# Issuing w2 and w1 ahead of wq at the head of a decode kernel's transfer queue

## The chip, the cores and the metric

The kernel runs on one core of a Trainium2 chip. The metric is device time in microseconds (us) of one execution, the median of several runs. The core has a matrix engine (TensorE, PE in the profile; PEld is its weight load), VectorE (DVE), ScalarE (ACT), GpSimd (POOL) and SyncE (SP), each with its own instruction stream, and 16 DMA engines that move data between device memory (HBM) and the on-chip buffer. Engines wait for one another, and for transfers, through semaphores.

## What is computed

One decode step with batch 4, one token each and width 576. A layernorm of x feeds two branches that are added to x: attention with 32 query heads over 16 key/value heads of 128, on the last 2048 of 8192 cached positions, and a mixing MLP. Cut to what matters here (all weights and inputs are bf16):

```python
xn = layernorm(x)                                   # (4, 1, 576)
# branch A
q = (xn @ wq).reshape(B, 1, 32, 128)                # wq (576, 4096)
k, v = k_cache[:, :, -2048:, :], v_cache[:, :, -2048:, :]
p = softmax(q k^T * 128**-0.5);  o = p v            # 2 query heads per KV head
a = o @ wo                                          # wo (4096, 576)
# branch B, on xn
h = gelu(layernorm(xn) @ w1)                        # w1 (576, 576)
hs = shift_along_sequence(h) @ w2                   # w2 (576, 576); shifts by 1 and 2, zeros moved in
x1 = xn + hs
b = x1 + gelu(layernorm(x1) @ w3) @ w4              # w3 (576, 4608), w4 (4608, 576)
out = x + a + b
```

With one token in the sequence every shift moves zeros in, so the operand of w2 in the kernel (hs_inT) is the zeroed tile of line 212. The product with w2 and the one with w1 are both executed.

## The kernel before

Everything but x comes in over one queue, SP's, as large transfers of 128 partitions each, in the order of SP's program: wq in three pieces (two of 2048 KB, each two of the four row groups, and a remainder of 512 KB), w2 and w1 (648 KB each), w3 in three pieces (two of 2304 KB and a remainder of 576 KB), then sixteen K tiles of 2048 KB, sixteen V tiles of 2048 KB with wo (4608 KB) among them, and w4 in five pieces. x is loaded by ACT's queue.

The buffers decide what may be issued when. K has four slots, and K tile g (from the fifth on) waits for the last transpose of tile g - 4 (the waits `T...` in line 237). V has four slots too. Before V comes, wq, w1 and w2 lie in V's slots, so the first V tiles wait for the product with w1, named `hT` (line 241). w3 lies in regB, which later holds the transposed K tiles. The first eight transfers and the first four K tiles wait for nothing.

What sets the order: every operation is added to one engine's list with a sort key (`add`, `add_dma`), and at the end each list is sorted by key and then by the order of adding (line 577). An engine runs its list in that order, and an instruction that waits holds all behind it on the same engine. The keys of the first transfers are -20 and -18 for the halves of wq, -15 for its remainder, -14 for w2, -13 for w1, -12 and -10 for the halves of w3, -8 for its remainder, then 0, 1, 2, ... for the K tiles.

PE's list at the head, in order: the transposes of xn (L294, L297) and of the second layernorm's result (L284); the q product with wq, 40 matmuls in five groups, the first two waiting for wq's first half, the next two for its second half, the last for its remainder (L316, `pe_q`); the eight transposes of q (L327); the product of hs_inT with w2 in two halves of 9 matmuls (`pe_hs`, L497), the product of xn2T with w1 (18 matmuls, L497, `hT`); the transposes of x1n (L294, L297); the product with w3, 60 matmuls in five groups, the first two waiting for w3's first half (24 matmuls), the next two for its second half, the last for its remainder (L528, `pe_h2`); four matmuls that zero the score banks (L341, `zeroS`), which wait for the gelu of the w3 product on ACT (L538); and then the loop over the K tiles: eight groups of eight transposes per tile (L352, `T0` to `T127`), copied out by DVE (L360) and ACT (L359), and the score matmuls (L368). After the scores come the softmax, sixteen groups of 64 matmuls with V (L449), the product with wo (L464) and the product with w4 (L464 for its first 14 row groups, L544 behind them), which ends the kernel with two small copies (L571, L572) and two output transfers.

The chain between the w2 product and the w3 product runs over DVE and ACT: x1 = xn + hs (L507), the third layernorm, transposes on PE, and the copy to x1nT (L512).

Of the kernel before, what the change touches and what calls it, by code (L numbers as in the profile page):

```python
# [38 lines left out]
def bass_parallel_sum__sliding_block_cached__mixer_s_mlp__decode_kernel(  # L39
# [22 lines left out]
    with ExitStack() as ctx:  # L62
# [3 lines left out]
        def sem(name):  # L66
            return ctx.enter_context(nc.semaphore(name))
# [15 lines left out]
        w1p = vring_t[:, _o:_o + 9 * HALF]  # L83
        _o += 9 * HALF
        w2p = vring_t[:, _o:_o + 9 * HALF]
# [79 lines left out]
        def add(engine, emit, waits=(), sig=None, key=0.0, loop=None):  # L165
            seqc[0] += 1
            prog[engine].append(Op(emit, waits, sig, key, seqc[0], loop))

        def add_dma(pairs, skey, waits=(), key=0.0, engine="sp"):
            if skey not in S:  # L170
                S[skey] = sem("s_" + "_".join(str(k) for k in (skey if isinstance(skey, tuple) else (skey,))))
            dma_count[skey] = dma_count.get(skey, 0) + 16 * len(pairs)

            def emit(e):
                for o_, i_ in pairs:
                    e.dma_start(o_, i_).then_inc(S[skey], 16)  # L176
            add(engine, emit, waits, None, key)
            return ("dma", skey, dma_count[skey])
# [42 lines left out]
        ev_wq.append(add_dma([(wqrag, rag_src(A_wq))], ("wq", 4), (), -15))  # L221
        def packed(w):
            return w.rearrange("r n -> (r n)").rearrange("(p e) -> p e", p=128)
        ev_w2 = add_dma([(w2p, packed(B_w2))], "w2", (), -14)
        ev_w1 = add_dma([(w1p, packed(B_w1))], "w1", (), -13)
        w3_src = B_w3[0:512, :].rearrange("(p r) n -> p r n", r=4)
        for r in (0, 2):
            ev_w3 += 2 * [add_dma([(w3main[:, r:r + 2, :], w3_src[:, r:r + 2, :])], ("w3", r), (), -12 + r)]
# [430 lines left out]
```

## Time and profile before

| | us |
|---|---|
| median of three runs | 214.77 |
| lowest and highest | 214.73, 214.99 |
| the profiled execution, whole | 214.88 |
| its span in the profile | 213.6 |
| PE busy | 138.9 (65%) |
| DVE busy | 87.3 (41%) |
| ACT busy | 59.3 (28%) |
| POOL busy | 12.0 (6%) |

How to read it. The profile is of one execution; times count from the start of its span. "L352" is line 352 of the kernel. The slices cut the span into 40 equal parts of 5.34 us; a digit is the busy share of a slice in tenths, 9 for 90% or more. A queue's share is the time that its packets took, as a share of 16 engines' span. The chain of waits goes back from the last instruction to what released it; its pieces are shown as start, duration, what. A row of the timeline has start, duration, engine, line, operation, output<-inputs with their shapes, the number of instructions, and in brackets the idle time ahead of it and what ended that. A row of transfers has the number, KB each, and the us from issue to landing. A row of the windows has for each engine its busy time and number of instructions, then the clock granted to PE (1.00 is full), the DMA share and GB/s.

### The profile page before, as it was taken

Reading aid. Unit: us, or ns where it says so; the run is one execution under the profiler, and the core shown is the slowest. Engines: PE = TensorE matmul, PEld = TensorE weight load, DVE = VectorE, ACT = ScalarE, POOL = GpSimd, SP = SyncE. Lnnn points to the kernel's source line nnn. Section 1 sums busy time; section 2 is a strip of 40 time slices with the busy share of each in tenths; the row PEclk is TensorE's granted clock in tenths of the full one; section 3 lists DMA queues with packets and bytes.
Section 4 is the critical chain, followed back from the end, with each engine's and each line's share of the span. In section 5 each row is a group of like instructions: output and inputs, shape, how many; then the busy total and the mean of one; then the engine's idle time right before and its main releaser. Section 6 shows DMA issues by size and latency. Waiting matters only on the chain.

```text
span 213.6 us, 5830 instructions
## 1 busy us (share of the span) xinstructions
PE 138.9 (65%) x2692; PEld 108.9 (51%) x2692; DVE 87.3 (41%) x162; ACT 59.3 (28%) x72; POOL 12.0 (6%) x39
## 2 busy tenths in 40 slices
PE   0089347999999994999999729823343443333585
PEld 0036123777777883788887503823343443333444
DVE  6725202566666664366666569611111112100000
ACT  2000302466665553266566654000000000000000
POOL 8501000000000100000000000000000000000000
PEclk9999855899999999699999995555555555555579
DMA  6999999999999999999999999999999999999993
GB/s 243 426 404 446 438 412 439 423 422 417 436 426 420 426 439 429 417 433 431 429 417 439 429 429 441 427 417 426 420 433 433 426 420 436 433 417 429 432 408 125
DMA packets 6657, 88.63 MB, mean 415 GB/s; under 512 B 748, under 2 KB 888, under 8 KB 1656
## 3 DMA queue, kind: packets, MB, share of 16 engines
q1 hardware_dynamic: 6632, 88.50, 97.8%
q8 instruction: 7, 0.11, 0.2%
q14 instruction: 2, 0.02, 0.0%
q10 hardware_dynamic: 16, 0.01, 0.0%
HBM read 88.49 MB, written 0.00 MB: 414 GB/s over the span
## 4 chain that ended last, share of the span: by engine, by line
DMA 52%; PE 39%; DVE 4%; issue 2%; SPq 1%; ACT 1%
PE ps L352 23%; DMA vring<-in_A_v_cache_dram 23%; DMA regB<-in_B_w_dram 12%; DMA kring<-in_A_k_cache_dram 8%; DMA vring<-in_B_w_dram 8%; PE ps L368 7%; PE ps L449 4%; PE ps L544 1%; PE ps L528 1%; DVE PTb L402 1%; SPq L176 1%; DVE rmax L394 1%; PE ps L341 1%; DVE regB L360 1%; ACT PTb L538 1%
## 5 line engine op out<-in xcount | busy, mean ns | idle before, releaser
L360 DVE COPY regB<-ps 128x1024 bf16<-128x1024 bf16 x80 | 52.4, 687 | 34.1 <-PE ps L352 32.3
L352 PEld LDWEIGHTS ps<-perm_k,kring 128*128 128x128 bf16 x1024 | 59.2, 100 | 11.6 <-issue 8.2
L352 PE MATMUL ps<-perm_k,kring 128*128 128x128 bf16 x1024 | 62.4, 222 | 3.2 <-DMA kring<-in_A_k_cache_dram 3.1
L359 ACT ACTIVATE regB<-ps 128x1024 bf16<-128x1024 bf16 x48 | 47.7, 1023 | 40.9 <-PE ps L352 40.9
L449 PE MATMUL ps<-PTg,vring 128*128 128x8 bf16 x1024 | 29.5, 168 | 39.0 <-DMA vring<-in_A_v_cache_dram 36.4
L449 PEld LDWEIGHTS ps<-PTg,vring 128*128 128x128 bf16 x1024 | 28.4, 104 | 40.1 <-DMA vring<-in_A_v_cache_dram 27.5
L457 DVE TENSOR_TENSOR PTb<-ps,PTb 128x32 bf16<-128x32 f32 x16 | 3.1, 192 | 56.1 <-PE ps L449 56.1
L368 PE MATMUL ps<-regB,Qs 128*32 128x512 bf16 x272 | 18.7, 396 | 4.6 <-issue 3.5
L554 ACT ACTIVATE P_sb<-ps 100x288 f32<-100x288 f32 x1 | 0.4, 411 | 75.8 <-PE ps L464 75.8
L368 PEld LDWEIGHTS ps<-regB,Qs 128*32 128x32 bf16 x272 | 6.6, 97 | 10.8 <-issue 6.4
L413 DVE TENSOR_TENSOR PTg<-PTs,bmask 128x512 bf16<-128x512 bf16 x16 | 10.7, 682 | 0.0
L390 POOL COPY Qs<-Qpad 128x128 bf16<-128x128 bf16 x16 | 4.6, 296 | 91.3 <-PE ps L368 82.0
L528 PE MATMUL ps<-regB,x1nT 128*32 128x432 bf16 (+1 forms) x60 | 4.4, 459 | 6.0 <-DMA regB<-in_B_w_dram 6.0
L541 DVE STREAM_TRANSPOSE h2T_sb<-PTb 128x1152 bf16<-128x1152 bf16 x1 | 1.4, 1379 | 11.4 <-ACT PTb L538 11.4
L528 PEld LDWEIGHTS ps<-regB,x1nT 128*32 128x32 bf16 x60 | 1.8, 122 | 8.0 <-DMA regB<-in_B_w_dram 6.6
L403 PE MATMUL ps<-PTb,perm_p 128*128 128x512 bf16 x4 | 2.4, 607 | 4.3 <-DVE PTb L402 4.1
L294 PE MATMUL ps<-ident_bf,xn_bf 4*128 4x4 bf16 x4 | 0.3, 166 | 7.5 <-DVE ragsrc L278 7.5
L571 DVE CAST out_sb<-ps 36x144 bf16<-36x144 f32 x1 | 0.3, 301 | 9.9 <-PE ps L544 9.9
L464 PE MATMUL ps<-kring,ORT 128*4 128x288 bf16 x64 | 4.0, 441 | 0.4 <-DVE ORT L478 0.4
L294 PEld LDWEIGHTS ps<-ident_bf,xn_bf 4*128 4x128 bf16 x4 | 0.2, 110 | 7.4 <-POOL ones_f L213 7.4
L316 PE MATMUL ps<-vring,xnT 128*32 128x512 bf16 x40 | 3.9, 571 | 0.0
L403 PEld LDWEIGHTS ps<-PTb,perm_p 128*128 128x128 bf16 x4 | 0.4, 104 | 6.3 <-DVE PTb L402 6.3
(99 smaller groups left out, 79.1 us busy)
## 6 DMA issues: line engine op xcount, KB each, us to landing
kring<-in_A_k_cache_dram SPq DMA_DIRECT2D x16, 2048.0 KB, 15.7
vring<-in_A_v_cache_dram SPq DMA_DIRECT2D x16, 2048.0 KB, 17.6
regB<-in_B_w_dram SPq DMA_DIRECT2D x2, 2304.0 KB, 23.5
kring<-in_A_wo_dram SPq DMA_DIRECT2D x1, 4608.0 KB, 23.6
vring<-in_A_wq_dram SPq DMA_DIRECT2D x2, 2048.0 KB, 9.6
vring<-in_B_w_dram SPq DMA_DIRECT2D x2, 2016.0 KB, 17.4
vring<-in_B_w_dram SPq DMA_DIRECT2D x2, 648.0 KB, 14.3
vring<-in_B_w_dram SPq DMA_DIRECT2D x1, 720.0 KB, 14.4
```

The lines of the kernel that those rows point to most:

```text
L316: ins = e.matmul(Qps[32 * j:32 * j + 32, k, :], lhsT=x_, rhs=w, start=(r == 0), stop=(r == 4), tile_position=(0, 32 * j))
L352: ins = e.transpose(tb[n % NTB][:, t, :], kring[:, g % NKS, 8 * k + t, :], perm_k[:])
L359: return "act", lambda e: e.activation(out=ktbuf[:, n % NKT], in_=src, func=ACTF.Copy)
L360: return "dve", lambda e: e.tensor_copy(out=ktbuf[:, n % NKT], in_=src)
L368: ins = e.matmul(Sps[32 * b:32 * b + 32, c4, :].rearrange("p (t i) -> p t i", t=16), lhsT=Qs[:, g % 4, b, :], rhs=kttile[:, t0:t0 + 16, b, :],
L390: P(lambda e, g=g: e.tensor_copy(out=Qs[:, g % 4], in_=Qpad[:, g]), waits=(["qT"] if g == 0 else []) + ([f"SC{g - 4}"] if g >= 3 else []), ...
L403: add("pe", lambda e, q=q, cs=cs: e.matmul(ps[:, q, :], lhsT=perm_p[:], rhs=PTb[:, cs], start=True, stop=True), waits=[f"PTb{q}"] + (["per ...
L413: add("dve", lambda e, g=g: e.tensor_tensor(out=PTg[:, g % NPG], in0=PTs[:, :, 2 * g:2 * g + 2].unsqueeze(2).to_broadcast([128, NT, B, 2]) ...
L449: ins = e.matmul(OTps(g), lhsT=vring[:, g % NVS, t, :], rhs=PTg[:, g % NPG, t].rearrange("p b e -> p (b e)"), start=(t == 0), stop=(t == N ...
L457: add("dve", lambda e, g=g: e.tensor_tensor(out=OTx[:, :, 2 * g:2 * g + 2, :], in0=OTps(g).rearrange("p (b e) -> p b e", b=B).unsqueeze(3) ...
L464: return e.matmul(ACC[h], lhsT=lhsT, rhs=rhs, start=start, stop=stop, tile_position=(k0, 32 * h))
L528: ins = e.matmul(H2ps[k][32 * j:32 * j + 32, :], lhsT=x_, rhs=w, start=(r == 0), stop=(r == 4), tile_position=(0, 32 * j))
```

## The change

Two sort keys. w2 gets -22 and w1 gets -21 in the place of -14 and -13, which puts both ahead of the first piece of wq (-20). The order of SP's first transfers becomes w2, w1, wq (three pieces), w3 (three pieces), K. The transfers themselves, their semaphores and every wait stay, and so do the programs of PE, DVE, ACT and POOL.

```diff
         ev_wq.append(add_dma([(wqrag, rag_src(A_wq))], ("wq", 4), (), -15))
         def packed(w):
             return w.rearrange("r n -> (r n)").rearrange("(p e) -> p e", p=128)
-        ev_w2 = add_dma([(w2p, packed(B_w2))], "w2", (), -14)
-        ev_w1 = add_dma([(w1p, packed(B_w1))], "w1", (), -13)
+        ev_w2 = add_dma([(w2p, packed(B_w2))], "w2", (), -22)
+        ev_w1 = add_dma([(w1p, packed(B_w1))], "w1", (), -21)
         w3_src = B_w3[0:512, :].rearrange("(p r) n -> p r n", r=4)
```

## The prediction

> **What bounds the kernel now.** I read the page's span, its slices and queue table first, then the chain of waits in order of time, then the transfers and instructions of the first 45 us one by one.
>
> ```profile
> span 213.6 us, 5830 instructions
> DMA  6999999999999999999999999999999999999993
> GB/s 243 426 404 446 438 412 439 423 422 417 436 426 420 426 439 429 417 433 431 429 417 439 429 429 441 427 417 426 420 433 433 426 420 436 433 417 429 432 408 125
> q1 hardware_dynamic: 6632, 88.50, 97.8%
> DMA 52%; PE 39%; DVE 4%; issue 2%; SPq 1%; ACT 1%
> ```
>
> The 16 DMA engines are at nine tenths or more in every slice but the first and the last. One queue, SP's, carries all the bytes that matter and fills 97.8% of their time. The chain gives PE 39%, but that is only how it was followed back; the question is whether the stream of transfers ever stops for PE. The chain's pieces:
>
> ```profile
> 3.76 26.01 DMA regB<-in_B_w_dram
> 29.77 0.04 issue
> 29.81 3.10 PE ps L528 x33
> 32.91 0.02 issue
> 32.93 1.26 ACT PTb L538 x3
> 34.20 0.05 issue
> 34.24 1.89 PE ps L341 x4
> ...
> 191.08 17.48 DMA vring<-in_B_w_dram
> 208.56 0.04 issue
> 208.60 3.17 PE ps L544 x88
> ```
>
> At the head PE waits until 29.77 for the second half of w3, and at the end it waits until 208.56 for a piece of w4. Between them stands the question of K4, the first transfer whose issue depends on PE (it overwrites K0's slot and waits for K0's last transpose):
>
> ```profile
> 42.25 0.54 SPq L176 DMA_DIRECT2D kring<-in_A_k_cache_dram  x1
> kring<-in_A_k_cache_dram SPq DMA_DIRECT2D x1, 2048.0 KB, 13.6
> ```
>
> It is issued at 42.25 and lands 13.6 us later. Its own 2048 KB need 4.87 us of the stream (below), so 13.6 - 4.87 = 8.7 us of other work lay ahead of it. PE would have to be 8.7 us later before the engines ran dry. So the time is the stream's: when it starts, how fast it runs, and the 3.17 us of PE and the output behind its end.
>
> **The change part by part.** No transfer is added, removed or resized, and PE, DVE, ACT and POOL keep their programs. SP issues w2 and w1 ahead of the three wq transfers. Today's head, with landing = start of the issue + time to landing (each issue's row is followed by the landing row of that transfer, whose last column is the us from issue to landing):
>
> ```profile
> 0.80 0.41 SPq L176 DMA_DIRECT2D vring<-in_A_wq_dram  x1
> vring<-in_A_wq_dram SPq DMA_DIRECT2D x1, 2048.0 KB, 7.4
> 1.27 0.88 SPq L176 DMA_DIRECT2D vring<-in_A_wq_dram  x2
> vring<-in_A_wq_dram SPq DMA_DIRECT2D x1, 2048.0 KB, 11.8
> 1.73 0.42 SPq L176 DMA_DIRECT2D vring<-in_A_wq_dram  x1
> vring<-in_A_wq_dram SPq DMA_DIRECT2D x1, 512.0 KB, 12.6
> 2.19 0.53 SPq L176 DMA_DIRECT2D vring<-in_B_w_dram  x1
> vring<-in_B_w_dram SPq DMA_DIRECT2D x1, 648.0 KB, 13.8
> 2.77 0.44 SPq L176 DMA_DIRECT2D vring<-in_B_w_dram  x1
> vring<-in_B_w_dram SPq DMA_DIRECT2D x1, 648.0 KB, 14.8
> 3.25 0.46 SPq L176 DMA_DIRECT2D regB<-in_B_w_dram  x1
> regB<-in_B_w_dram SPq DMA_DIRECT2D x1, 2304.0 KB, 21.0
> 4.76 0.62 SPq L176 DMA_DIRECT2D kring<-in_A_k_cache_dram  x1
> kring<-in_A_k_cache_dram SPq DMA_DIRECT2D x1, 2048.0 KB, 31.3
> ```
>
> The landings are wq's first half 8.20, its second half 1.27 + 11.8 = 13.07 (the first of that line's two issues), its remainder 14.33, w2 15.99, w1 17.57, w3's first half 24.25, K0 36.06. They come in issue order and close up: 13.07 - 8.20 = 4.87 us for 2048 KB (431 GB/s), 1.66 and 1.58 us for 648 KB each (about 410 GB/s). So the queue is served first in, first out, and a transfer behind another pays only its bytes. Its lead (issue to first effect) is 7.4 - 4.87 = 2.53 us and is seen once.
>
> (1) The stream from w3 on. The five transfers ahead of w3 have the same bytes in any order, so w3 lands at 24.25 and 29.77 and K0 at 36.06, as today: 0.
>
> (2) wq lands later by what is put ahead of it: 17.57 - 14.33 = 3.24 us, so 11.44, 16.31 and 17.57. What waits for it:
>
> ```profile
> 11.63 3.94 PE L316 MATMUL ps<-vring,xnT 128*32 128x512 bf16 x40
> 17.00 2.37 PE L497 MATMUL ps<-vring,hs_inT 128*4 128x288 bf16 x18
> 22.70 0.15 DVE L512 COPY x1nT<-ps 128x24 bf16<-128x24 bf16 x1
> 24.29 1.33 PE L528 MATMUL ps<-regB,x1nT 128*32 128x432 bf16 x24 [1.78 <-DMA regB<-in_B_w_dram]
> 29.81 3.07 PE L528 MATMUL ps<-regB,x1nT 128*32 128x432 bf16 x36 [4.19 <-DMA regB<-in_B_w_dram]
> ```
>
> PE runs in order, and the hs product stands behind the q product and its transposes in PE's program although w2 now comes first. So w2's early landing (about 0.80 + 2.53 + 1.6 = 4.9) is used by nobody, and the whole train moves: the q product can still start at 11.63 on the first half but ends at 11.63 + 3.94 + 3.24 = 18.8; hs starts at 17.00 + 3.24 = 20.2; x1nT is ready at 22.85 + 3.24 = 26.1. Today PE then idles 1.78 us for w3's first half and 4.19 us for the second. After the change the first 24 products of L528 start at 26.1 instead of 24.29 and take 1.33 us, or 24/36 of 3.07 = 2.05 us at the lower clock: done by 27.4 to 28.2, still 1.6 to 2.3 us ahead of 29.77. Behind PE on this train are the copies of q for POOL, the table load and the first gelu on ACT, which nobody needs before the second gelu at 32.93: covered as well. Cost: 0, hidden by the wait for w3's second half. If that cover were gone, whatever exceeds it would push K4's issue, which has the 8.7 us above; the clock's turns shift PE in the same cover. 0.
>
> (3) SP's queue. Eight issues lie between 0.80 and 4.76 in both orders, one every 0.47 to 0.58 us; each K issue stands behind the same number of them. 0.
>
> (4) The start of the stream. This is the part with no row of its own: today a 2048 KB transfer opens the stream, then a 648 KB one will.
>
> ```profile
> 0.00:4.00 4.00, 0.00 (x0) 0.00 (x0) 2.09 (x5) 1.28 (x1) 3.33 (x11) 1.00 0.57 177
> 40.00:60.00 20.00, 19.01 (x324) 15.92 (x322) 13.08 (x21) 11.86 (x12) 1.18 (x4) 1.00 1.01 426
> ```
>
> The last column is GB/s. In the first 4 us the stream moved 4 x 177/426 = 1.66 us worth of bytes; 0.80 us pass before the first issue, so starting up costs 4 - 0.80 - 1.66 = 1.54 us. The gain is bounded by that, all of it saved: -1.5. The loss is bounded by paying it a second time for the second small transfer: +1.5. Between them I take 0: w1 is issued 0.47 us after w2, while w2 alone occupies the engines for 1.6 us, so when w2's bytes run out the next ones have been asked for long since, and the nearest rows (w2 and w1 landing 1.66 and 1.58 us apart in mid-stream) show no gap at a boundary between small transfers.
>
> The Trainium skill's page "DMA: Bandwidth & Descriptors", in "Rules for kernel authors", asks for at least 1 MiB per transfer for full bandwidth, which speaks against opening with two of 648 KB. By it each would pay a fixed part again; by the landings 1.66 and 1.58 us apart, 410 against 431 GB/s, they lose some 5% of their own 1.6 us, and lose it in either order.
>
> **The sum.** Span 213.6 + 0 + 0 + 0 + 0 = 213.6; the profiled execution took 214.88 us, so 1.28 us lie around the span. That execution is 0.11 above the median of the three runs (214.77, from 214.73 to 214.99). The forecast for the median is 214.77, written 214.8.
>
> **The rivals.**
> *Slower: the head of the stream starves.* w2's 1.6 us are over before w1's descriptors have reached all engines, and w1's before wq's. It decides from the point where a transfer is ready for the engines more than 1.6 us later than the one issued 0.47 us before it. The price is what the issue step can leave open, about 0.45 us at each of two boundaries: 214.77 + 0.9 = 215.7. For it: a first-microseconds rate of 177 GB/s shows that the engines are not fed at full pace at once. Against it: with the same lead of 2.53 us for each, w1's bytes are ready at 1.27 + 2.53 = 3.80, before w2's end at about 4.9. The page's rule on size, above, points the same way.
>
> *Faster: the small opening starts up better.* Smaller rows per partition finish their first round sooner, and part of the 1.54 us is saved; half of it gives 214.77 - 0.77 = 214.0. For it: a DMA share of 0.57 in the first 4 us with 177 GB/s, where a share of 1.01 gives 426: 0.57 would be worth 240, so the engines were busy for part of it without moving bytes at their pace. Against it: if that time is the lead to the first bytes, it doesn't depend on what comes first.
>
> *Slower: the train of q does reach the path.* If x1nT came not 3.2 but over 5.6 us later (24.29 - 22.85 = 1.44 of the first wait, and the 4.19 of the second), PE would pass 29.77; from 8.7 us beyond that the stream would wait too, and each further microsecond costs one. For 1 us more, 215.8. Nothing in the rows makes 3.2 into 5.6 + 8.7 = 14.3.
>
> **How the numbers follow.** What a measurement of this kernel can't tell from no change is about 0.2%, 0.43 us, so 214.34 to 215.20 counts as the same. Forecast 0.62; starving head 0.16; better start 0.18; the train on the path, with other small losses of the stream's pace, 0.04. That makes faster 0.18, same 0.62, slower 0.20. The range takes in most of both small cases' halves: below to 214.2, above to 215.6; outside it stay the far ends of the bounds, 213.3 and 216.3.
>
> **What would show it.** Right: SP's first rows in the new order; wq landing near 11.4, 16.3 and 17.6; the hs product starting near 20.2 and the first L528 group near 26.1; and yet the second L528 group starting at 29.8, the first transposes at 36.2, K4's issue within a microsecond of 42.25, and the last PE group at 208.6. Wrong in part (4): w3's and K0's landings and the last PE group shifted together by the same amount, which is then the start of the stream, up or down. Wrong in part (2): the second L528 group starting later than w3's landing. The forecast falls if the landings stay and the end moves: then something set the pace between 42 and 208 us that I took for hidden.

## The result and the profile after

| | before | changed |
|---|---|---|
| median of 22 executions each, us | 214.76 | 215.13 |
| lowest and highest | 214.58, 215.06 | 214.72, 215.55 |
| ratio, with its 95% interval | | 1.0016 (1.0010 to 1.0022) |
| profiled execution, whole / span | 214.88 / 213.6 | 215.18 / 213.9 |

The change costs 0.37 us, 0.16%. That lies inside the predicted range and inside the 0.2% that were called "the same", though the interval of this comparison leaves out a ratio of 1. The spread has grown with the median: 9 of the 22 executions lie in the range of the kernel before, and 13 are above its highest.

The first K transposes of the kernel before, from its chain of waits:

```profile
36.22 1.89 PE ps L352 x16
```

The changed kernel's span, the piece of its chain of waits that ends in a K tile, the first K transposes, and the timeline's last PE group:

```profile
span 213.9 us, 5830 instructions
5.54 31.07 DMA kring<-in_A_k_cache_dram
36.74 1.88 PE ps L352 x16
...
208.97 3.09 PE L544 MATMUL ps<-vring,h2T_sb 128*4 128x144 bf16 x88
```

Before, K0 landed at 36.06, the transposes started at 36.22 and the last group at 208.60. All three are later, by 0.55, 0.52 and 0.37 us. The loss is there before the first K tile is used, and nothing is added behind it. The head of SP's queue, issue rows followed by landing rows:

```profile
0.80 0.41 SPq L176 DMA_DIRECT2D vring<-in_B_w_dram  x1
vring<-in_B_w_dram SPq DMA_DIRECT2D x1, 648.0 KB, 4.0
1.27 0.41 SPq L176 DMA_DIRECT2D vring<-in_B_w_dram  x1
vring<-in_B_w_dram SPq DMA_DIRECT2D x1, 648.0 KB, 5.2
1.73 1.22 SPq L176 DMA_DIRECT2D vring<-in_A_wq_dram  x1
vring<-in_A_wq_dram SPq DMA_DIRECT2D x1, 2048.0 KB, 10.1
2.99 0.43 SPq L176 DMA_DIRECT2D vring<-in_A_wq_dram  x1
vring<-in_A_wq_dram SPq DMA_DIRECT2D x1, 2048.0 KB, 13.7
3.46 0.43 SPq L176 DMA_DIRECT2D vring<-in_A_wq_dram  x1
vring<-in_A_wq_dram SPq DMA_DIRECT2D x1, 512.0 KB, 14.5
```

The new order is there. w2 lands at 4.80 and w1 at 6.47, but wq's first half lands at 11.83, 5.36 us behind w1, where 2048 KB need 4.87: half a microsecond is lost at this boundary, going by the landings; what the stream as a whole loses is worked out below. From there on the pace is the old one (16.69 - 11.83 = 4.86). One issue, the third, took 1.22 us instead of 0.42. PE behind it:

```profile
11.84 1.90 PE L316 MATMUL ps<-vring,xnT 128*32 128x512 bf16 x16 [0.16 <-DMA vring<-in_A_wq_dram]
16.75 2.75 PE L316 MATMUL ps<-vring,xnT 128*32 128x512 bf16 x24 [3.01 <-DMA vring<-in_A_wq_dram]
20.93 2.37 PE L497 MATMUL ps<-vring,hs_inT 128*4 128x288 bf16 x18
26.93 1.16 PE L528 MATMUL ps<-regB,x1nT 128*32 128x432 bf16 x24 [0.49 <-DVE x1nT L512]
30.34 3.07 PE L528 MATMUL ps<-regB,x1nT 128*32 128x432 bf16 x36 [2.26 <-DMA regB<-in_B_w_dram]
43.16 0.53 SPq L176 DMA_DIRECT2D kring<-in_A_k_cache_dram  x1
```

PE's train is late as forecast (26.93 for the first w3 products, which were at 24.29) and still waits 2.26 us for w3's second half. K4 is issued at 43.16, 0.9 us later than before, inside the 8.7 us that it has.

### The profile page after: what moved, and what is told of

The parts are those of the page before. It is cut to its first block, busy times and chain, and to the rows that moved or that the text cites. A ratio compares the mean times of both kernels' runs of the same rounds, so it can differ in the third digit from the quotient of the medians.

```text
span 213.9 us, 5830 instructions
## 1 busy us (share of the span) xinstructions
PE 138.3 (65%) x2692; PEld 108.0 (50%) x2692; DVE 87.2 (41%) x162; ACT 59.6 (28%) x72; POOL 11.9 (6%) x39
## 4 chain that ended last, share of the span: by engine, by line
DMA 48%; PE 41%; DVE 4%; issue 3%; SPq 2%; ACT 1%
DMA vring<-in_A_v_cache_dram 25%; PE ps L352 23%; DMA kring<-in_A_k_cache_dram 23%; PE ps L368 7%; PE ps L449 6%; PE ps L464 3%; SPq L176 2%; PE ps L544 2%; DVE PTb L402 1%; DVE rmax L394 1%; DVE regB L360 1%; DVE PTs L410 1%; PE ps L425 0%; ACT P_sb L399 0%; ACT P_sb L554 0%
## 5 line engine op out<-in xcount | busy, mean ns | idle before, releaser
L352 PEld LDWEIGHTS ps<-perm_k,kring 128*128 128x128 bf16 x1024 | 58.1, 98 | 11.8 <-issue 8.5
L316 PE MATMUL ps<-vring,xnT 128*32 128x512 bf16 x40 | 4.7, 629 | 3.2 <-DMA vring<-in_A_wq_dram 3.2
L316 PEld LDWEIGHTS ps<-vring,xnT 128*32 128x32 bf16 x40 | 1.2, 133 | 5.8 <-DMA vring<-in_A_wq_dram 4.4
```

What stands on the lines that cost most here:

```text
L316: ins = e.matmul(Qps[32 * j:32 * j + 32, k, :], lhsT=x_, rhs=w, start=(r == 0), stop=(r == 4), tile_position=(0, 32 * j))
L352: ins = e.transpose(tb[n % NTB][:, t, :], kring[:, g % NKS, 8 * k + t, :], perm_k[:])
```

## The experiments

A transfer is moved in rows, one for each of its 128 partitions, which makes eight for each of the 16 DMA engines if they are shared evenly. The profile's windows are too coarse here, since they count a row of 16 KB whole where it starts. So two tables are worked out from the trace's records of single rows (start, duration, bytes), for one profiled execution of each kernel. The first has the rate of SP's queue in GB/s, each row's bytes spread evenly over its duration, in steps of 0.5 us from the time at the top, and the MB moved by 8.0 us:

```
                       1.5   2.0   2.5   3.0   3.5   4.0   4.5   5.0   5.5   6.0   6.5   7.0   7.5   MB
before                  20   156   227   308   404   418   425   424   427   431   430   430   428   2.26
changed                 31   102   295   422   406   421   406   385   356   335   359   412   422   2.18
e1_again                14    81   233   383   409   418   423   417   424   430   432   431   430   2.26
e9_again                14    77   244   414   415   418   423   415   411   376   407   426   423   2.23
e10_wq_wait             16    93   228   400   411   421   424   423   408   401   423   430   427   2.25
e12_rem_again           17   165   413   412   406   418   415   416   421   408   417   426   432   2.38
e11_three_small         35   174   333   388   418   421   373   310   318   386   400   406   400   2.18
e5_cols_head            30   117   359   399   401   305   277   240   339   373   398   404   411   2.03
```

The changed kernel reaches its pace half a microsecond earlier than the kernel before (422 against 308 at 3.0) and then falls back to 335 between 5.0 and 7.0, where the small rows end and wq's rows begin. The second table has the times, in us, at which rows end near the head and near the end of the stream: for w3's remainder (128 rows of 4608 bytes) the first row, the 120th, the last and the mean of all, for w4's 256 rows of 16128 bytes the mean and the last, and the whole time of the same execution:

```
                     w3's remainder                     w4, 16128 bytes
                  first    120th     last     mean       mean     last     whole
before            27.79    29.43    30.72    28.70     202.55   208.13    214.88
changed           27.78    29.90    31.23    28.91     202.73   208.48    215.18
e1_again          27.66    29.43    31.09    28.65     202.49   208.22    214.94
e9_again          27.74    29.59    30.81    28.73     202.55   208.25    215.00
e10_wq_wait       27.61    29.45    30.70    28.67     202.53   208.16    214.90
e2_big_first      27.80    29.46    30.70    28.70     202.55   208.04    214.72
e12_rem_again     27.50    29.20    30.57    28.45     202.25   207.87    214.63
e11_three_small   27.88    29.73    30.77    28.86     202.67   208.05    214.79
e5_cols_head      28.08    30.12    31.28    29.22     203.05   208.82    215.73
```

Three things can be read from it.

- The whole time is the last row of w4 and 6.68 to 6.91 us more, in every line (6.65 to 6.91 over all fourteen profiles).
- What the stream as a whole loses at the head stays lost. By 8.0 us the changed kernel has moved 2.176 MB where the kernel before has moved 2.264. The 0.088 MB that are missing need 0.20 us at 430 GB/s, and its mean row is 0.21 us later at w3's remainder and still 0.18 later at w4. e12 has moved 0.119 MB more, worth 0.28 us, and its means are 0.25 and 0.30 us earlier.
- The rest is how far the latest rows lag behind the mean. The changed kernel's last row of w4 is 0.35 us later, twice as much as its mean. e11 had lost nearly as much by 8.0 us (0.082 MB) and its mean is 0.12 later at w4, but its last row is 0.08 earlier, and that execution took 214.79.

The last row of w3's remainder is a poor measure of the head. In the kernel before, the changed kernel and e1 the last eight rows follow one another at about 0.18 us, as one engine's rows do, while the other 120 have ended by 29.43, 29.90 and 29.43. Followed from row to row, each starting where the one before it ends, the engine that is late had carried a packet of 16384 bytes of another queue, which the page of the profile calls "instruction" (7 packets, 0.11 MB in the whole execution): at 21.57 for 1067 ns in the kernel before, at 25.54 and 26.05 in the other two. The row of w3 behind it took 1184 ns, where its neighbours take 686. K0's landing seems to go by the same engine: eight rows of 611 ns behind 30.72, 31.23 and 31.09 end at 35.61, 36.12 and 35.98, and K0 landed 0.45 to 0.49 us later each time.

**First comparison: is it the opening, or the late q product?** Theory 1 was the starving head, theory 2 that the train of q reaches the path after all. Four kernels are compared on one chip with 33 executions of the kernel before (214.72 to 215.05, median 214.90). The three comparisons ran on three different chips, each with the kernel before beside them.

e1_again is the changed kernel, unaltered.

> The changed kernel once more, unaltered, for a second profile and as the anchor of this comparison. Theory 1 (the head starves): 215.1 (+0.37 over before); in its trace the landings of w1 and of wq's first half lie over 5.3 us apart, where 2048 KB need 4.87, and w3's second half and K0 land 0.3 to 0.6 us later than in the kernel before (29.77, 36.06). It is open whether SP's third issue takes 1.22 us again or 0.4. Theory 2 (the late q product, 3 us later, is what costs, through K4's issue and what follows): 215.1 too, but with w3 and K0 landing as before.

e2_big_first puts w2 and w1 behind wq's first half instead of ahead of it:

```diff
-ev_w2 = add_dma([(w2p, packed(B_w2))], "w2", (), -14)
-ev_w1 = add_dma([(w1p, packed(B_w1))], "w1", (), -13)
+ev_w2 = add_dma([(w2p, packed(B_w2))], "w2", (), -19)
+ev_w1 = add_dma([(w1p, packed(B_w1))], "w1", (), -18.5)
```

> wq's first half opens the stream, then w2, w1, wq's second half and its remainder. The q product is as late as in the changed kernel, since wq's remainder again lands last of the five (about 17.6). Theory 1: no small transfer opens, so 214.76 as before (within 0.1), w3's second half at 29.8, K0 at 36.1. Theory 2: 215.1 as in the changed kernel.

e3_rem_first moves wq's remainder to the head of the kernel before:

```diff
-ev_wq.append(add_dma([(wqrag, rag_src(A_wq))], ("wq", 4), (), -15))
+ev_wq.append(add_dma([(wqrag, rag_src(A_wq))], ("wq", 4), (), -21))
```

> wq's remainder (512 KB) opens the stream, then the halves of wq, w2, w1. The q product ends when it did in the kernel before (all of wq has landed by 14.3). Theory 1: a small opening of 1.2 us of data before a large transfer, one boundary instead of two: 214.8 to 215.2, with K0 landing 0 to 0.5 us later than 36.06. Theory 2: 214.76 as before.

e4_w2_only moves only w2:

```diff
-ev_w2 = add_dma([(w2p, packed(B_w2))], "w2", (), -14)
+ev_w2 = add_dma([(w2p, packed(B_w2))], "w2", (), -22)
```

> Only w2 (648 KB) is moved to the head; w1 stays behind wq. The q product is 1.6 us later than before, half of what the change does. Theory 1: one small transfer ahead of a large one: 214.8 to 215.2; if what counts is the time that the small ones cover (1.6 us here, 3.2 in the changed kernel) against the arrival of the large one's rows, the hole is not smaller than in the changed kernel. Theory 2: about half of the loss, 214.9.

| | median, us | lowest to highest of 11 | ratio to before (interval) |
|---|---|---|---|
| e1_again | 214.95 | 214.78 to 215.44 | 1.0011 (1.0002 to 1.0020) |
| e2_big_first | 214.91 | 214.72 to 215.13 | 1.0002 (0.9993 to 1.0011) |
| e3_rem_first | 214.59 | 214.49 to 214.78 | 0.9987 (0.9978 to 0.9996) |
| e4_w2_only | 214.83 | 214.65 to 214.96 | 0.9996 (0.9987 to 1.0005) |

The ratio goes by all executions and is not the quotient of the two medians, which for e1_again is 1.0002.

Theory 2 is out. The timeline of e2_big_first, with the first K transposes and the last group from its chain of waits:

```profile
28.59 0.67 PE L528 MATMUL ps<-regB,x1nT 128*32 128x432 bf16 x12 [0.48 <-DVE x1nT L512]
...
36.19 1.06 PE ps L352 x16
...
208.53 3.11 PE ps L544 x88
```

Its w3 products start at 28.59, still later than in the changed kernel (26.93), and yet the K transposes (36.19) and the last group (208.53) are where they were before the change. A train that is 4.3 us late costs nothing.

The opening matters, but not by being small. One short transfer at the head is harmless (w2 alone) or gains 0.31 us (wq's remainder), against the expectation of 0 to 0.4 us of loss. And e1_again, profiled in an execution of 214.94, shows what the changed kernel does when all goes well: its chain of waits has the third issue at the usual length,

```profile
1.72 0.42 SPq L176
vring<-in_A_wq_dram SPq DMA_DIRECT2D x1, 2048.0 KB, 9.7
```

its rate has no dip, and wq's first half lands at 1.72 + 9.7 = 11.42, 4.95 us behind w1 (6.47). The expected 5.3 us between them was wrong for this execution. K0 still landed 0.38 us later than before (36.44). That is not the head's doing: the mean row of w3's remainder is 0.05 us earlier than before and 120 of the 128 rows have ended by 29.43 as before, but the engine that carried the instruction packet ends at 31.09 instead of 30.72.

**Second comparison: how fast are transfers made ready?** The idea after the first comparison was that the queue makes one transfer after another ready, about 1.9 us each, so that two transfers of 1.6 us of data run out before the third is there. Kernel before: 27 executions, median 214.84. e5 and e6 cut w2 and w1 in halves at the head of the changed kernel, by columns and by partitions (shown for w2):

```diff
-ev_w2 = add_dma([(w2p, packed(B_w2))], "w2", (), -22)
+ev_w2 = add_dma([(w2p[:, c:c + 1296], packed(B_w2)[:, c:c + 1296]) for c in (0, 1296)], "w2", (), -22)     # e5
+ev_w2 = add_dma([(w2p[p:p + 64, :], packed(B_w2)[p:p + 64, :]) for p in (0, 64)], "w2", (), -22)           # e6
```

> The changed kernel with w2 and w1 each loaded in two halves by columns: four transfers of 324 KB, 128 rows each, open the stream. Theory 1, made exact from the runs so far (the queue makes one transfer after another ready, about 1.9 us each: the first rows of the second start at 3.6 us, of the third at 5.4 to 6.1): wq's first half is now fifth, ready at about 9 us, while the four small ones hold only 3.2 us of data, gone by 5.6. So a hole of 3 to 4 us, K0 landing at 39 to 40, time 218 to 219. Rival (the third issue of 1.22 us in the first trace of the changed kernel was what starved the engines, and each issue costs 0.45): the fifth is issued by 2.7, ready by 4.6, no hole, 214.8 to 215.0.

> The same four pieces cut the other way: two halves of 64 partitions for each of w2 and w1, so twice the transfers of the changed kernel but the same number of rows (4 x 64). If making ready goes by transfer: as e5, 218 to 219. If it goes by rows: each takes half of 1.9 us, wq's first half is ready at 5.4 to 6.1 as in the changed kernel, time 215.0 to 215.2.

e7 has the column halves in their old place (keys -14 and -13):

> The kernel before with the same column halves of w2 and w1 in their old place behind wq, as the control of e5: what the split itself costs. Theory 1: by then five or more transfers are ready ahead, no hole: 214.8 to 215.0 (rows of 2592 bytes a few per cent slower over 3.2 us: +0.1).

e8 issues w1 from ACT's queue in the changed kernel:

```diff
-ev_w1 = add_dma([(w1p, packed(B_w1))], "w1", (), -21)
+ev_w1 = add_dma([(w1p, packed(B_w1))], "w1", (), -99, engine="act")
```

> The changed kernel with w1 issued by ACT's queue right behind x instead of SP's, so that wq's first half is second on SP's queue. If making ready is a matter of each queue: wq is ready at 3.7, before the small ones are through at 5.5, no hole, the gain of the small opening stays: 214.4 to 214.6. If the two queues share it: as the changed kernel, 214.95 to 215.15.

| | median, us | lowest to highest | ratio to before (interval) |
|---|---|---|---|
| e5_cols_head | 215.26 | 214.96 to 216.25 (10) | 1.0024 (1.0013 to 1.0035) |
| e6_parts_head | 217.34 | 217.26 to 217.37 (4) | 1.0118 (1.0102 to 1.0133) |
| e7_cols_old | 215.04 | 214.87 to 215.12 (10) | 1.0009 (1.0000 to 1.0018) |
| e8_w1_act | 214.89 | 214.77 to 215.09 (11) | 1.0003 (0.9994 to 1.0012) |

The idea of 1.9 us per transfer falls: four short transfers should have cost over 3 us and cost 0.42, of which the split itself accounts for 0.20 (e7, with its small rows away from the head, is a little above the 214.8 to 215.0 expected). The rival expected no loss beyond 215.0 and is wrong as well. The dip is there, though, longer and deeper (240 at 5.0 in the table), and the spread is the widest of all the kernels here. e8 lies between its two expectations and decides nothing. e6 doesn't test what it was meant to test, because its transfers are slow in themselves. The windows of the changed kernel (first two rows) and of e6_parts_head (last two), whose last column is GB/s:

```profile
3.00:5.00 2.00, 0.00 (x0) 0.00 (x0) 2.00 (x4) 0.00 (x0) 2.00 (x3) 1.00 1.02 415
5.00:7.00 2.00, 0.00 (x0) 0.00 (x0) 1.58 (x9) 0.20 (x1) 1.93 (x8) 1.00 1.13 417
```

```profile
3.00:5.00 2.00, 0.00 (x0) 0.00 (x0) 2.00 (x4) 0.00 (x0) 2.00 (x3) 1.00 1.06 257
5.00:7.00 2.00, 0.00 (x0) 0.00 (x0) 1.58 (x9) 0.20 (x1) 1.93 (x8) 1.00 1.00 228
```

Transfers to 64 partitions run at little over half the pace with the engines fully busy (DMA share 1.06 and 1.00), so the 2.5 us that e6 costs come from the slow transfers.

**Third comparison: is it the third issue's lateness?** Theory 3 took the 1.22 us of that issue as the cause. Kernel before: 33 executions, 214.73 to 215.04, median 214.89.

> The changed kernel a third time. Its two profiles so far: one of 215.18 us with a third issue of 1.22 us and first wq rows of 741 to 1182 ns, one of 214.94 us with a third issue of 0.42 us and first wq rows of 611 ns. Theory 3 (wq's first half is made ready about when the 3.2 us of small rows run out, and in some executions its third issue is late, so that its rows start up like those at the head of a stream): this profile is one of the two kinds, first rows at 611 ns with a run below 215.0, or over 700 ns with a run above 215.1. If the two don't go together, theory 3 falls.

e10 holds that issue back until POOL has zeroed xnT:

```diff
-ev_wq += 2 * [add_dma([(wqmain[:, r:r + 2, :], wq_src[:, r:r + 2, :])], ("wq", r), (), -20 + r)]
+ev_wq += 2 * [add_dma([(wqmain[:, r:r + 2, :], wq_src[:, r:r + 2, :])], ("wq", r), ["xnT_zero"] if r == 0 else (), -20 + r)]
```

> The changed kernel with wq's first half held back on SP until POOL has zeroed xnT (3.81 us), instead of being issued at 1.73: a lateness of 2.1 us made on purpose. All later transfers wait behind it. Theory 3: lateness of that issue is what costs; the small rows are gone by 5.5, the rows of wq start 1.9 us or more behind the issue, at 5.8 to 7.6, and the stream loses 0.3 to 2 us: 215.3 to 217, w3 and K0 landing later by as much. Rival (the opening of small rows costs in itself, whatever wq's issue does): as the changed kernel, 214.95 to 215.15.

e11 puts wq's remainder ahead of w2 and w1 in the changed kernel (key -23), three short transfers in all:

> wq's remainder, w2 and w1 open, then the halves of wq: three small transfers with 4.4 us of data instead of two with 3.2. wq's first half is issued one step (0.46 us) later, and has 1.2 us more of data ahead of it. Theory 3: it is ready in time in all executions, no dip, and the better start of the 4096-byte rows stays: 214.5 to 214.75, close together. Rival (small openings cost in themselves, more the more there are): 215.2 or more.

e12 is e3 again:

> wq's remainder alone at the head, once more (214.59 against 214.90 of the kernel before in its first comparison, 0.9987 with an interval of 0.9978 to 0.9996): the gain stands if this is 0.15 to 0.4 us under the kernel before again. Full rate by 2.5 us in its trace, against 3.25 in the kernel before.

| | median, us | lowest to highest | ratio to before (interval) |
|---|---|---|---|
| e9_again | 214.91 | 214.71 to 215.13 (11) | 1.0000 (0.9991 to 1.0009) |
| e10_wq_wait | 214.81 | 214.68 to 215.04 (10) | 0.9997 (0.9988 to 1.0006) |
| e11_three_small | 215.10 | 214.64 to 215.54 (11) | 1.0009 (0.9999 to 1.0019) |
| e12_rem_again | 214.63 | 214.55 to 214.80 (11) | 0.9989 (0.9980 to 0.9998) |

Theory 3 falls. SP's rows of e9_again and, behind it, of e10_wq_wait, with e10's first K transposes and last group:

```profile
1.73 1.29 SPq L176
```

```profile
3.84 1.29 SPq L176 DMA_DIRECT2D vring<-in_A_wq_dram  x3
...
36.22 1.89 PE ps L352 x16
...
208.65 3.11 PE ps L544 x88
```

In e9 the third issue is as long as in the first profile, and the execution took 215.00, near the kernel before; its first rows of wq took 608 to 887 ns, neither of the two kinds expected. In e10 wq's first half is issued 2.1 us late, and its first row starts at 5.50 by the trace's records, right behind the last small rows, as it does when it is issued at 1.73 (5.42 in the changed kernel, 5.56 in e1). Nothing is lost by it: 214.81 is below both expectations, 215.3 to 217 and 214.95 to 215.15. So the third issue has two microseconds to spare, whatever its length. e11 speaks against theory 3 too, which expected its executions close together at 214.5 to 214.75; they lie between 214.64 and 215.54. e12 came out as expected, 0.26 us under the kernel before.

**What is shown and what stays open.** Executions above 215.06, the highest of the 115 of the kernel before, by the number of short transfers in a row at the head:

- none, with w2 and w1 behind a large transfer (e2): 1 of 11;
- one (e3, e4, e12): 0 of 33;
- one on SP's queue, with the other on ACT's (e8): 1 of 11;
- two (changed, e1, e9): 13 + 5 + 1 = 19 of 44;
- three (e11): 6 of 11;
- four (e5): 8 of 10, against 4 of 10 where the same four pieces stand behind wq (e7);
- two with a pause of 2.1 us behind them (e10): 0 of 10.

Shown is that several short transfers one behind another at the very head bring a loss, that it comes in some executions only, and, in the profiled ones, that the bytes missing by 8 us come back as a later mean row at the end, to which the lag of the latest rows is added. Not on every occasion, though: in the third comparison the changed kernel (e9) lost nothing against the kernel before. What inside the queue slows the rows near 5 us is open, and so is what decides how far the latest rows lag and why the share of the longer executions of the changed kernel differs from one measurement to the next (13 of 22, 5 of 11, 1 of 11). The number of short transfers is not separated from their bytes and the length of their rows either, which change with it. That issuing all the rest at once behind the short ones has a part in it is suggested by e10, but ten executions against e9's eleven in the same comparison (214.81 and 214.91, overlapping intervals) don't settle it.

A version that beats both kernels came out of it: wq's remainder at the head, everything else in the old order, 0.31 and 0.26 us under the kernel before in two comparisons. Its first issue and landing, first K transposes and last group:

```profile
0.81 0.41 SPq L176 DMA_DIRECT2D vring<-in_A_wq_dram  x1
vring<-in_A_wq_dram SPq DMA_DIRECT2D x1, 512.0 KB, 3.4
...
36.08 1.89 PE ps L352 x16
...
208.35 3.13 PE ps L544 x88
```

It is at 413 GB/s from 2.5 us on, where the kernel before has 227, stays above 400, and ends the last w4 row of 16128 bytes at 207.87 instead of 208.13.

## Why the prediction held, point by point

- What bounds the kernel: held. In all fourteen profiles the whole time is the last row of w4 and 6.65 to 6.91 us more, and a lateness of PE of 4.3 us (e2) did not reach it.
- Part (1), the stream from w3 on at 0: wrong by 0.55 us in the profiled execution (K0 at 36.61 instead of 36.06), and by 0.21 in the mean row of w3's remainder. Its argument was that the same bytes lie ahead; they do, but the pace at which the head moves them had changed, and that belongs to part (4).
- Part (2): held. The train came at 26.93 instead of the predicted 26.1, 0.4 us of the difference being wq's own landings (11.83, 16.69, 17.96 against 11.44, 16.31, 17.57), and was hidden with 2.26 us to spare; e2, at 28.59, shows that still more would have been.
- Part (3): the number was wrong and the 0 was right. One issue took 1.22 us and K0 was issued 0.8 us later; e10 shows that 2.1 us are free there.
- Part (4), the start of the stream, taken at 0 between -1.5 and +1.5, is the term that was mis-sized. It measured +0.37 in the result, +0.05 in the first and +0.02 in the third comparison, as differences of medians, with single executions up to 0.8 above the kernel before. Its two sides are both real: a faster start and a dip behind the second short transfer. In the profiled execution the changed kernel has moved 0.07 MB more than the kernel before by 4.0 us, and 0.09 less by 8.0. The reason given for 0, that the next rows have been asked for long since, holds (e10), but it does not exclude the dip. The 0 is therefore in part luck: it stood for the middle between two bounds, and the median came near it because a gain and a loss that the prediction couldn't size offset each other in part.
- The two numbers that part (4) rests on are readings of something else. The 177 GB/s count rows whole that had only started: spread over their durations, 0.56 MB had moved by 4.0 us and not 0.71, so that starting up cost about 1.9 us and not 1.54. And the lead of 2.53 us is not the time to the first bytes: in the kernel before the first row starts at 1.82, 1.0 us behind the start of the issue, and the first rows of 16 KB then take up to 1495 ns where later ones take 611.
- The rival that the head starves had the place and the sign right and the mechanism wrong: lateness of the next issue was to decide, and e10 made it late without a loss. Its price of 0.9 was more than twice the median loss of 0.37.
- The rival that a small opening starts up better was right about the start and wrong about this kernel: its gain shows where one short transfer opens and a long one follows, 0.26 to 0.31 of the 0.77 us that it was priced at.
- The rule of at least 1 MiB for a transfer, from the Trainium skill's page "DMA: Bandwidth & Descriptors" (section "Rules for kernel authors"), does not order these kernels: the one with 512 KB at the head is the fastest. The same section's advice not to split a transfer into disjoint partition halves agrees with e6, where such halves ran at 257 and 228 GB/s against 415 and 417.

## What to carry to other kernels

In a kernel bound by one stream of transfers, count what a reordering does to the first few microseconds of the stream, and to its latest engine, before looking at who uses the data: a product that is 3 to 4 us late in the shadow of a later transfer costs nothing, while what the stream has not moved by 8 us is still missing at its end. One short transfer first and a long one behind it started this stream soonest; several short ones in a row reached the pace as soon and fell back from it. A difference of 0.1 to 0.2% that comes from some executions only needs dozens of them: three measurements of the same two kernels gave 1.0016, 1.0011 and 1.0000.

## What was unexpected

The rows of one transfer end up to 3 us apart (27.79 to 30.72 for w3's remainder in the kernel before). Part of that is that each engine has eight rows to move, and the last 1.3 us are a single engine that had carried an instruction packet: the other rows have ended by 29.43. So a landing tells of the latest engine and not of the stream's mean. And a transfer of 324 KB to 64 partitions moved at little more than half the pace of one to 128, with as many engines busy.
